# Linear attention with top-1 experts on one core: results of conditional slots moved behind the next branch, three more row buffers, tail weights asked for later

## The chip, the cores and the metric

The kernel runs on one core of a Trainium2 chip. Five engines work side by side, each through its own list of instructions in order: PE (TensorE, the matrix multiplier), ACT (ScalarE), DVE (VectorE), POOL (GpSimd) and SP (SyncE, which here issues the transfers from and to DRAM). An engine that waits for a semaphore holds up everything behind it in its own list. The metric is the device time of one execution in microseconds; the figure of the kernel before is the median of three runs.

## The reference

Attention with positive features is computed for 8 batches, 8 heads and 576 tokens of width 64. Each of the resulting 4608 rows of 512 numbers then goes through one of 8 experts, the one with the largest gate logit.

```python
def phi(x):
    proj = np.einsum('bhsd,df->bhsf', x, w_phi)
    proj = proj - np.max(np.abs(proj), axis=-1, keepdims=True)
    return np.concatenate([np.exp(proj), np.exp(-proj)], axis=-1)
q_p, k_p = (phi(q), phi(k))
kv = np.einsum('bhsf,bhsd->bhfd', k_p, v)
z = np.sum(k_p, axis=2)
num = np.einsum('bhsf,bhfd->bhsd', q_p, kv)
den = np.einsum('bhsf,bhf->bhs', q_p, z)[..., None] + 1e-06
x = num / den                      # 4608 rows of 512
...
logits = x @ w_gate + modality_bias[modality_id]
e_idx = np.argmax(logits, axis=1)
...
for e in range(E):
    mask = e_idx == e
    out[mask] = gate_w[mask, None] * (np.maximum(x[mask] @ w1[e], 0.0) @ w2[e])
```

All is float32. Each expert has weights of 512x1024 and 1024x512, 4 MB together. How many rows an expert gets is known only when the gate has been computed.

## The kernel before, in words

**Attention** runs over 16 quarter groups. Its steps stand in one hand-written list (`ORDER`), under which the lists of SP, PE, ACT and DVE are made. The last step of a block of 128 tokens is `rows()`: DVE multiplies the transposed result by the reciprocal denominators into a buffer `xs` of 128x512 (line 645; `xs_l` is the leftover block of a group), and SP stores it to the DRAM array `x` (line 650). These buffers come from the pool `x1`, which has two of them.

**Routing** counts the rows of each expert and writes lists of (gate weight, row number) to DRAM. The work is cut into *slots* of 256 rows of one expert. Slots 0 to 13 always run. Slots 14 to 20 stand in nested branches `if n > p` (line 1031), where n comes out of the routing; here slots 0 to 17 run. Four small slots are interleaved in slots 6 to 12; the remaining rows of an expert would go into further *small slots*, in branches of their own (`small()`, line 1039 on). With these inputs there is none: the first of their branches jumps over all of them.

**A slot** (`two(p)`) does the following. Weights and tokens are float32, and each is split into a high and a low part, so that a product is made of three matmuls. PE does 96 matmuls of the first layer (line 807), 0.12 us apart, then eight transposes of the next slot's tokens (line 780), then 48 matmuls of the second layer (line 824), 0.23 us apart. Ahead of that:

- SP asks for the weights in four transfers of 1 MB into the buffers `raw` (line 750; two for each layer). A pair is asked for again when its buffers have been split: the second layer's pair of slot p+1 and the first layer's pair of slot p+2 are asked for in slot p. ACT casts the high part (line 770), DVE subtracts the low part (line 772, `l<-raw,h`).
- `mload` lets SP read a slot's list of rows, `me<-lst` (line 724), two slots ahead. `gather` lets POOL fetch these rows, `xg<-x,me` (line 728), once PE has transposed what was in the buffer before.
- At the end, in `second`, DVE scales the two halves of the result by the gate weight into `os` (line 855), and POOL scatters each to the output (`scatter`, line 734).

The weights of small slots go into buffers of their own. `sload(0)` and `sload(1)`, 4 MB each, are asked for just ahead of slot 13. At line 1031 and at line 1039 each engine evaluates the branch by itself, from the counts that it has loaded into its registers. Where a branch is not entered, an engine still performs the semaphore steps that the others rely on.

Of the kernel before, what the change touches and what calls it, by code (L numbers as in the profile page):

```python
# [8 lines left out]
F32 = mybir.dt.float32  # L9
F32R = mybir.dt.float32r  # L10
BF16 = mybir.dt.bfloat16
I32 = mybir.dt.int32
U32 = mybir.dt.uint32
AF = mybir.ActivationFunctionType
ALU = mybir.AluOpType
AX = mybir.AxisListType
PSUM = bass.MemoryType.PSUM
SP, PE, ACT, DVE, POOL = (getattr(mybir.EngineType, e) for e in ("SP", "PE", "Activation", "DVE", "Pool"))

P = 128  # L20
# [5 lines left out]
D, E, F = 512, 8, 1024  # L26
# [6 lines left out]
EARLY, SURE, MOST = 6, 14, 21  # L33
FIX = (1, 3)
FIRST = 6
NME = 8
# [17 lines left out]
class Line:  # L54


    def __init__(self, tc):
        self.tc, self.last, self.free = tc, None, []
# [279 lines left out]
class Attention:  # L338
# [3 lines left out]
    def __init__(self, tc, ci, c, w_phi):  # L342
        self.tc, self.nc = tc, tc.nc
        nc = tc.nc
        self.st, self.rd, self.lg = {}, {}, {}
        self.wp = c.tile([P, P], F32, name="wp")
        for j, e in enumerate((nc.scalar, nc.gpsimd)):
            e.dma_start(self.wp[64 * j:64 * j + 64], w_phi)
        self.c, self.ident = c, ci.tile([P, P], F32, name="ident")
# [291 lines left out]
    def rows(self, T, r0, xp, rd, w, x):  # L641

        nc = self.nc
        xs = w.tile([P, 2, 4, 64], F32, tag="xs", name=f"xs{T}")
        nc.vector.tensor_tensor(xs, xp.rearrange("p (i g d) -> p i g d", i=2, d=64),  # L645
                                rd.rearrange("p g i -> p i g").unsqueeze(3).to_broadcast([P, 2, 4, 64]), ALU.mult)
        xs = xs.rearrange("p i g d -> p (i g d)")
        for j, r in enumerate(r0):
            m = P // len(r0)
            nc.sync.dma_start(x[r:r + m, :], xs[m * j:m * j + m])  # L650
# [39 lines left out]
def run(stages):  # L690
    for _ in stages:
        pass


class Experts:
# [131 lines left out]

    def two(self, p):

        j = p - FIRST  # L830
        for k in range(4):
            if j % 2 == 0 and 0 <= j < 2 * sum(FIX):
                self.fixed(j // 2, k)
            run(self.mm1(k))
            self.wsplit(p, 4 + k)
            next(self.side, None)
            if p < 4:
                next(self.side, None)
        self.wload(p + 1, 1)
        if p + 1 < MOST:  # L840
            self.turn(self.XG)
            run(self.xsplit())
        self.xload(p + 2)
        for t in range(2):
            run(self.second(p, t))
        self.wload(p + 2, 0)

    def second(self, p, t):

        nc, me = self.nc, self.ME[p % NME]  # L850
        pp = self.mm2(p, t)
        yield
        for j in range(2):
            self.wsplit(p + 1, 2 * t + j)
        nc.vector.tensor_scalar(self.OS[t], pp, me[:, t, 0:1].bitcast(F32), None, ALU.mult)  # L855
        self.scatter(me[:, t, 1:2], self.OS[t], D)
        next(self.side, None)
        yield

    def raws(self, s):  # L860

# [138 lines left out]
    def slots(self):  # L1000
        tc, nc = self.tc, self.nc
        why = "the plan makes it within these bounds"
        for p in range(1, SURE):
            j, odd = divmod(p - FIRST + 2, 2)
            if p in range(SURE - 6, SURE - 2):
                for s in range(2):
                    self.smeta(2 * (p - SURE + 6) + s)
            if p == FIRST - 2:
                for i in range(sum(FIX)):
                    self.fmeta(i)  # L1010
            if 0 <= j < sum(FIX):
                self.fload(j, odd)
                if not odd:
                    self.fgather(j)
            if p == SURE - 2:
                self.n, *self.others = (
                    nc.values_load(self.route.n[0:1, i:i + 1], min_val=a, max_val=b, skip_runtime_bounds_check_because=why)
                    for i, a, b in ((0, SURE, MOST), (1, 0, E), (2, 0, E), (3, 0, E)))
            if p == SURE - 1:
                for s in range(2):  # L1020
                    self.sload(s)
                for s in range(3):
                    self.gather(self.rows(s), self.MS[:, 0, s, 1:2])
            self.two(p)
            if 0 <= j < sum(FIX) and odd:
                self.turn(self.HX.unsqueeze(1))
                self.xplain()
            if p == SURE - 1:
                self.turn(self.rows(0).unsqueeze(1))
                self.xplain()  # L1030
        with ExitStack() as st:
            for p in range(SURE, MOST):
                st.enter_context(tc.If(self.n > p))
                self.two(p)

    def small(self):
        tc = self.tc
        more, ones, halves = self.others
        with ExitStack() as st, tc.manual_schedule(engines={SP, PE, ACT, DVE, POOL}):
            for s in range(E):  # L1040
                st.enter_context(tc.If(more > s))
                for t in (3, 4) if s == 0 else (s + 2,) if 3 <= s < E - 2 else ():
                    self.gather(self.rows(t), self.MS[:, 0, t, 1:2])
                if s == 0:
                    with tc.If(more > 3):
                        self.sload(3)
                with tc.If(ones > s) as k:
                    self.one(s)
                with k.Else():
                    with tc.If(halves > s) as k:  # L1050
                        self.part(s, 2)
                    with k.Else():
                        self.part(s, 4)
                if s + 4 < E:
                    with tc.If(more > s + 4):
                        self.sload(s + 4)
# [50 lines left out]
def program(tc, qT, kT, vm, vt, w_phi, w_gate, mod, bias, w1, w2, out):  # L1107
    nc = tc.nc

    def pool(stack, name, side="left", bufs=1, space=bass.MemoryType.SB):  # L1110
        return stack.enter_context(tc.tile_pool(name=name, bufs=bufs, side=side, space=space, reuse_waits="tile"))

    with ExitStack() as ctx:
# [3 lines left out]
        c = pool(ctx, "c")  # L1117
        left, lkv, right, feat, pl, pr, split = (ExitStack() for _ in range(7))
        rw = pool(left, "rw")
        att = Attention(tc, c, pool(left, "ac"), w_phi)  # L1120
# [3 lines left out]
        ex = Experts(tc, att.ident, route, lst, x, w1, w2, out)  # L1124
        ex.ME = [c.tile([P, 2, 2], I32, name=f"me{i}") for i in range(NME)]
        ex.XG = c.tile([P, 2, D], F32, name="xg")
        ex.MS = c.tile([P, 3, E, 2], I32, name="ms")
        ex.MG = c.tile([P, sum(FIX), 2], I32, name="mg")
        ex.IX = [c.tile([P, 1], I32, name=f"ix{i}") for i in range(2)]
        x1 = pool(left, "x1", bufs=2)  # L1130
# [93 lines left out]
        for j, (u, q) in enumerate(order):  # L1224
            k = seen[u, q] = seen.get((u, q), 0) + 1
# [9 lines left out]
        with tc.manual_schedule(engines={SP, PE, ACT, DVE}):  # L1235
# [9 lines left out]
            for j, o in enumerate(order):  # L1245
# [17 lines left out]
                    ex.OS = [b_.tile([P, D], F32, name=f"os{i}") for i in range(2)]  # L1263
                if j == end["lkv"]:
                    lkv.close()
                if o[0] in ("W4", "W5", "W6", "W7") and "h2" not in ex.W:
                    ex.weights(pool(split, "mC", "right"), ("h2", "l2"))
                step(*o)
# [60 lines left out]
```

## Time and profile before

| | us |
|---|---|
| device time, median of 3 runs | 800.19 |
| lowest and highest of these | 799.51, 800.84 |
| the profiled execution | 793.71 |
| its span, first to last instruction | 791.9 |

In the profiled execution PE was busy for 752.0 us, DVE for 552.6, ACT for 449.6 and POOL for 278.9; the mean granted clock of PE was 0.988 of full speed. The kernel read 144.97 MB and wrote 19.55 MB. Attention with the routing fills the first 336 us or so, the slots the rest. The page's times are in microseconds; a row of a timeline has the start, the length, the engine, the line, the operation with output and inputs and, in brackets, how long the engine stood idle before it and what ended that. Rows with SPq, POOLq, DVEq and the like are those of an engine's instruction sequencer: transfers asked for, semaphores and branches. A gap in the sequence of PE's rows costs time only if nothing later would have waited anyway.

### The profile page before, as it was taken

How to read it: one execution, taken by the hardware profiler on the slowest of the kernel's cores; microseconds unless marked ns; L12 is line 12 of the kernel's file. 1: busy time of each engine (PE TensorE's matmuls, PEld its weight loads, DVE VectorE, ACT ScalarE, POOL GpSimd, SP SyncE). 2: the span in 40 equal slices, each digit the busy share in tenths (PEclk: the TensorE clock that was granted, in tenths of full speed). 3: DMA queues.
4: the chain of work that ended last, by engine and by line, in shares of the span. 5: the costliest groups of instructions: out<-in, count | busy, mean ns of one | idle time of the engine just before them, and what ended most of it. 6: DMA issues, size and time to landing. Idle time of an engine off the chain costs nothing. (4 is left out here: it accounts for less than half of the span.)

```text
span 791.9 us, 18459 instructions
## 1 busy us (share of the span) xinstructions
PE 752.0 (95%) x7332; PEld 581.5 (73%) x7332; DVE 552.6 (70%) x815; ACT 449.6 (57%) x675; POOL 278.9 (35%) x163
## 2 busy tenths in 40 slices
PE   6899999989989999979999999999999999989994
PEld 4456555546555555869999987988999889879993
DVE  4889987988788996969765673566546746545752
ACT  3888688767768787535453453445434544435450
POOL 3543434445774784242221231132132321222221
PEclk9999999999999999999999999999999999989997
DMA  8444343336574517669657984867787949956540
GB/s 235 119 119 138 85 138 111 112 101 183 99 133 94 145 28 245 206 198 352 215 199 285 402 314 134 347 217 288 275 304 252 361 164 409 412 183 248 201 174 29
DMA packets 56676, 163.39 MB, mean 206 GB/s; under 512 B 22057, under 2 KB 24173, under 8 KB 43776
## 3 DMA queue, kind: packets, MB, share of 16 engines
q1 hardware_dynamic: 47584, 142.42, 53.7%
q0 software_dynamic: 7792, 18.96, 6.8%
q8 instruction: 62, 1.02, 0.6%
q10 hardware_dynamic: 1200, 0.68, 0.4%
q14 instruction: 38, 0.31, 0.1%
HBM read 144.97 MB, written 19.55 MB: 208 GB/s over the span
## 5 line engine op out<-in xcount | busy, mean ns | idle before, releaser
L770 ACT CAST h<-raw 128x1024 fp32r<-128x1024 f32 x148 | 149.8, 1050 | 107.6 <-PE p L824 56.6
L772 DVE TENSOR_TENSOR l<-raw,h 128x1024 fp32r<-128x1024 f32 x148 | 175.6, 1221 | 47.0 <-ACT h L770 34.4
L502 POOL PARTITION_ALL_REDUCE mq<-d x32 | 129.2, 4040 | 127.5 <-ACT d L476 74.0
L807 PE MATMUL p<-xh,l 128*128 128x256 f32 x576 | 163.9, 285 | 2.8 <-DVE l L772 2.8
L807 PE MATMUL p<-xh,h 128*128 128x256 f32 x576 | 164.7, 287 | 1.1 <-DVE xs L645 1.1
L807 PE MATMUL p<-xl,h 128*128 128x256 f32 x576 | 163.5, 284 | 0.0
L807 PEld LDWEIGHTS p<-xh,l 128*128 128x128 f32 x576 | 110.9, 193 | 5.1 <-DVE l L772 3.0
L807 PEld LDWEIGHTS p<-xh,h 128*128 128x128 f32 x576 | 111.0, 193 | 2.9 <-DVE xs L645 1.3
L728 POOL DMA_INDIRECT xg<-x,me x40 | 55.3, 1383 | 160.7 <-PE pt L780 80.0
L807 PEld LDWEIGHTS p<-xl,h 128*128 128x128 f32 x576 | 111.1, 193 | 0.4
L811 ACT ACTIVATE hh<-p 128x512 fp32r<-128x512 f32 x72 | 42.7, 594 | 112.8 <-PE p L807 112.8
L824 PE MATMUL p<-h,hh 128*128 128x512 f32 x272 | 105.9, 398 | 0.0
L813 DVE SCALAR_TENSOR_TENSOR hl<-p,hh 128x512 fp32r<-128x512 f32 x72 | 49.4, 688 | 80.9 <-ACT hh L811 80.9
L824 PE MATMUL p<-l,hh 128*128 128x512 f32 x272 | 104.3, 392 | 0.0
L824 PE MATMUL p<-h,hl 128*128 128x512 f32 x272 | 104.1, 393 | 0.0
L510 ACT ACTIVATE qp<-d 128x1152 f32<-128x1152 f32 x64 | 71.1, 1161 | 16.8 <-DVE d L505 14.5
L734 POOL DMA_INDIRECT out_dram<-os,me x36 | 39.8, 1106 | 113.7 <-DVE os L855 85.3
L459 ACT ACTIVATE kp<-dk 128x1024 f32<-128x1024 f32 x64 | 64.5, 1063 | 5.2 <-DVE dk L455 5.1
L555 DVE TENSOR_TENSOR kp<-kp 128x1024 f32<-128x1024 f32 x48 | 66.5, 1391 | 0.9 <-PE kvT L522 0.8
L522 PE MATMUL kvT<-kp,va 128*32 128x256 f32 x1024 | 59.2, 380 | 3.9 <-DVE xs L645 1.8
L824 PEld LDWEIGHTS p<-h,hl 128*128 128x128 f32 x272 | 51.5, 189 | 11.0
L824 PEld LDWEIGHTS p<-l,hh 128*128 128x128 f32 x272 | 51.6, 190 | 10.4
(251 smaller groups left out, 1119.8 us busy)
## 6 DMA issues: line engine op xcount, KB each, us to landing
raw<-in_w_dram SPq DMA_DIRECT2D x100, 1024.0 KB
qt<-in_qT_dram SPq DMA_DIRECT2D x30, 288.0 KB
va<-in_vm_dram SPq DMA_DIRECT2D x16, 512.0 KB
x<-xs SPq DMA_DIRECT2D x32, 256.0 KB
kt<-in_kT_dram SPq DMA_DIRECT2D x15, 512.0 KB
kt<-in_kT_dram SPq DMA_DIRECT2D x16, 64.0 KB
vb<-in_vt_dram SPq DMA_DIRECT2D x16, 64.0 KB
x<-xs_l SPq DMA_DIRECT2D x8, 128.0 KB
```

The source lines that it names most:

```text
L459: nc.scalar.activation(kp[:, :, :, s, :].rearrange("p t a f -> p a t f"), dk, AF.Exp, scale=sc)
L502: self.line(nc.gpsimd.partition_all_reduce(mq.rearrange("p a s -> p (a s)"), d.rearrange("p a s -> p (a s)"), P, bass_isa.ReduceOp.absmax))
L510: nc.scalar.activation(q["qp"][:, 2 * pr:2 * pr + 2, i, :], d, AF.Exp, scale=sc)
L522: nc.tensor.matmul(pt[pr][32 * c:32 * c + 32], va[:, pr, t, 32 * c:32 * c + 32], kp[:, pr * 4 + t, c // 2, :, :], start=t == 0, stop=False ...
L555: nc.vector.tensor_tensor(kv4[:, :, t], kv4[:, :, t], kv4[:, :, u], ALU.add)
L728: g = self.nc.gpsimd.indirect_dma_start(xg, None, self.x[:rows, :], IndirectOffsetOnAxis(ix.bitcast(U32), 0), bounds_check=rows - 1, oob_i ...
L770: nc.scalar.copy(h, r)
L772: nc.vector.tensor_tensor(l, r, h, ALU.subtract)
L807: nc.tensor.matmul(pp[:, j], a[:, cc, f], b[:, cc], start=i == 0, stop=i == 11)
L811: nc.scalar.activation(self.HH[:, sl], pp, AF.Relu)
L813: nc.vector.scalar_tensor_tensor(self.HL[:, sl], pp, 0.0, self.HH[:, sl], ALU.max, ALU.subtract)
L824: nc.tensor.matmul(pp, a[:, f, tk], b[:, f], start=i == 0, stop=i == 23)
```

## The change

Three edits, in the words of the code:

1. When the pools that attention's value loads used are closed, a new pool `xo` with three buffers is opened on their place. From then on `rows()` counts its calls, and three calls out of five take a buffer of `xo`, two one of the old pair. What is written and stored is the same.
2. From slot 13 on the last part of a slot, the two `os` rows and their scatters, is no longer written at the end of the slot but in a function `result` that is called at the start of the next slot, behind that slot's branch. The last slot that runs has its results in `small()`, in both ways of its branch: ahead of the small slots if there are some, and in the `Else` if there are none. There the slot's number is not known, so each slot from 13 on copies its list, 128x4 words, to a tile `ml`.
3. `sload(0)` is called after slot 13's `two`, `sload(1)` inside the branch for small slots, if there are more than one of them.

```diff
@@ rows
+        if self.out:
+            self.turns += 1
+            if self.turns % 5 > 1:
+                w = self.out[0]
         xs = w.tile([P, 2, 4, 64], F32, tag="xs", name=f"xs{T}")
...
@@ two
+        if p >= SURE - 1:
+            for t in range(2) if p >= SURE else ():
+                self.result(self.ME[(p - 1) % NME], t)
+            self.nc.vector.tensor_copy(self.ML, self.ME[p % NME])
...
@@ second
-        nc.vector.tensor_scalar(self.OS[t], pp, me[:, t, 0:1].bitcast(F32), None, ALU.mult)
+        if p < SURE - 1:
+            self.result(me, t)
+        next(self.side, None)
+        yield
+
+    def result(self, me, t):
+        self.nc.vector.tensor_scalar(self.OS[t], self.P2[t], me[:, t, 0:1].bitcast(F32), None, ALU.mult)
         self.scatter(me[:, t, 1:2], self.OS[t], D)
-        next(self.side, None)
-        yield
...
@@ slots
             if p == SURE - 1:
-                for s in range(2):
-                    self.sload(s)
                 for s in range(3):
                     self.gather(self.rows(s), self.MS[:, 0, s, 1:2])
             self.two(p)
...
             if p == SURE - 1:
                 self.turn(self.rows(0).unsqueeze(1))
                 self.xplain()
+                self.sload(0)
...
@@ small
+        with self.tc.manual_schedule(engines={SP, PE, ACT, DVE, POOL}):
+            with self.tc.If(self.others[0] > 0) as k:
+                for t in range(2):
+                    self.result(self.ML, t)
+                self.lists()
+            with k.Else():
+                for t in range(2):
+                    self.result(self.ML, t)
+
+    def lists(self):
         tc = self.tc
         more, ones, halves = self.others
-        with ExitStack() as st, tc.manual_schedule(engines={SP, PE, ACT, DVE, POOL}):
+        with ExitStack() as st:
             for s in range(E):
-                st.enter_context(tc.If(more > s))
+                if s:
+                    st.enter_context(tc.If(more > s))
...
-                    with tc.If(more > 3):
-                        self.sload(3)
+                    for t in (1, 3):
+                        with tc.If(more > t):
+                            self.sload(t)
...
@@ program
                 if j == end["lkv"]:
                     lkv.close()
+                    att.out.append(pool(left, "xo", bufs=3))
```

How the lists of the engines change is shown at three places. The first is DVE's list around the end of slot 0 (`os` of slot 0; `raw_0` and `raw_2` are weights of slot 1; `ns4l`, `al`, `cetl` belong to the routing). Before:

```order
L855 TENSOR_SCALAR os_3927<-pt_3869,me_73 128x512
L219 TENSOR_TENSOR ns4l<-ns4l,fi4l 128x8
L219 TENSOR_TENSOR al<-tri,ns4l 128x8x8
L645 TENSOR_TENSOR xs_0_4337<-xp_0_4254,rd_4_4071 128x512
L241 TENSOR_REDUCE cetl<-al 128x8
L645 TENSOR_TENSOR xs_l<-xl_4262,rd_8_4076 128x512
L772 TENSOR_TENSOR l_3862<-raw_0_123,h_3861 128x1024 x2
```

After:

```order
L869 TENSOR_SCALAR os_3928<-pt_3870,me_73 128x512
L649 TENSOR_TENSOR xs_0_4341<-xp_0_4258,rd_4_4075 128x512
L649 TENSOR_TENSOR xs_l<-xl_4266,rd_8_4080 128x512
L776 TENSOR_TENSOR l_3863<-raw_0_124,h_3862 128x1024 x2
L219 TENSOR_TENSOR ns4l<-ns4l,fi4l 128x8
L219 TENSOR_TENSOR al<-tri,ns4l 128x8x8
L776 TENSOR_TENSOR l_4058<-raw_2_3967,h_4057 128x1024 x2
```

The two `xs` rows moved up behind `os`, and the weight splits up behind them; the routing rows now stand later.

The second is SP's list in slot 13; the transfers of weights come in pairs, and one row of each pair stands here. `raw_0_123` and `raw_2_3963` (after: `raw_0_124` and `raw_2_3967`) are the weights of the slots, the `raw` with a last number from 4391 to 4402 those of small slots, `me_80` is the list of slot 15. Before (slot 15's first pair follows):

```order
L750 DMA raw_0_123<-in_w_dram 128x2048
...
L750 DMA raw_0_4391<-in_w_dram 128x2048
...
L750 DMA raw_2_4393<-in_w_dram 128x2048
...
L750 DMA raw_0_4395<-in_w_dram 128x2048
...
L750 DMA raw_2_4397<-in_w_dram 128x2048
...
L750 DMA raw_2_3963<-in_w_dram 128x2048
...
L724 DMA me_80<-lst 128x2x2
```

After:

```order
L754 DMA raw_0_124<-in_w_dram 128x2048
...
L754 DMA raw_2_3967<-in_w_dram 128x2048
...
L728 DMA me_80<-lst 128x2x2
...
L754 DMA raw_0_124<-in_w_dram 128x2048
...
L754 DMA raw_0_4396<-in_w_dram 128x2048
...
L754 DMA raw_2_4398<-in_w_dram 128x2048
```

The list and slot 15's first pair now come ahead of the small slots' weights, of which two pairs are left.

The third is the border of slots 13 and 14 on DVE (`me_78` is the list of slot 13, line 1031 and 1042 the branch of slot 14). Before:

```order
L855 TENSOR_SCALAR os_3926<-p_4411,me_78 128x512
L855 TENSOR_SCALAR os_3927<-p_4412,me_78 128x512
L1031 COMPARE_AND_BRANCH
L772 TENSOR_TENSOR l_4054<-raw_2_3963,h_4053 128x1024 x2
L772 TENSOR_TENSOR l_4054<-raw_3_3964,h_4053 128x1024 x2
```

After:

```order
L1042 COMPARE_AND_BRANCH
L869 TENSOR_SCALAR os_3927<-p_4416,me_78 128x512
L869 TENSOR_SCALAR os_3928<-p_4417,me_78 128x512
L837 COPY ml<-me_79 128x4
L776 TENSOR_TENSOR l_4058<-raw_2_3967,h_4057 128x1024 x2
L776 TENSOR_TENSOR l_4058<-raw_3_3968,h_4057 128x1024 x2
```

The two results of slot 13 moved behind the branch, and the copy of slot 14's list was added. On POOL the same was done with the scatters; at the end of POOL's list, where the branches of slots 14 to 20 close, the last of them and what follows was, before:

```order
L1031 COMPARE_AND_BRANCH
L757 COMPARE_AND_BRANCH
L757 UNCONDITIONAL_BRANCH x2
L734 DMA out_dram<-os_3926,me_77 4608x512
L734 DMA out_dram<-os_3927,me_77 4608x512
L1031 UNCONDITIONAL_BRANCH
```

and is after, with the flags and the branch of the small slots ahead of the scatters:

```order
L1042 ISA
L1042 UNCONDITIONAL_BRANCH
L1029 TENSOR_LOAD nslots x3
L1049 COMPARE_AND_BRANCH
L738 DMA out_dram<-os_3927,ml 4608x512
L738 DMA out_dram<-os_3928,ml 4608x512
```

The scatters that stood ahead of the closing branches stand behind them.

## Rows read from the trace of the kernel before

**Rows 1.** The page, part 1: busy us (share of the span) xinstructions.

```profile
PE 752.0 (95%) x7332; PEld 581.5 (73%) x7332; DVE 552.6 (70%) x815; ACT 449.6 (57%) x675; POOL 278.9 (35%) x163
```

**Rows 2.** Slots 1, 2, 13, 14: length, busy, PEclk, DMA share, GB/s.

```profile
347.60:377.10 29.50, 25.57 (x156) 23.23 (x155) 26.45 (x85) 11.35 (x14) 6.63 (x7) 0.94 0.76 268
377.10:400.40 23.30, 23.30 (x153) 21.33 (x152) 18.52 (x34) 11.36 (x14) 5.59 (x4) 1.00 0.67 232
656.40:679.66 23.26, 23.26 (x154) 21.30 (x154) 11.73 (x15) 8.04 (x11) 2.11 (x3) 1.00 1.01 417
679.66:710.02 30.36, 26.34 (x155) 23.57 (x154) 14.44 (x16) 14.94 (x19) 6.75 (x6) 0.89 0.75 287
```

**Rows 3.** DVE timeline, slot 1: start, us, operation [idle before <-releaser].

```profile
342.36 0.75 DVE L855 TENSOR_SCALAR os<-pt,me 128x512 f32<-128x512 f32 x1 [0.26 <-PE pt L824]
...
349.18 0.69 DVE L645 TENSOR_TENSOR xs<-xp,rd 128x512 f32<-128x512 f32 x1 [5.81 <-DMA x<-xs]
...
351.46 0.69 DVE L645 TENSOR_TENSOR xs_l<-xl,rd 128x512 f32<-128x512 f32 x1 [1.47 <-DMA x<-xs]
352.07 2.35 DVE L772 TENSOR_TENSOR l<-raw,h 128x1024 fp32r<-128x1024 f32 x2
```

**Rows 4.** Timeline of PE in slot 1.

```profile
349.93 0.39 PE L807 MATMUL p<-xh,h 128*128 128x256 f32 x1 [1.12 <-DVE xs L645]
...
353.34 0.58 PE L807 MATMUL p<-xh,l 128*128 128x256 f32 x1 [2.80 <-DVE l L772]
```

**Rows 5.** Timeline of SP's DMA issues, 318 to 360 us.

```profile
326.33 6.14 SPq L650 DMA_DIRECT2D x<-xs  x3
...
337.16 13.06 SPq L650 DMA_DIRECT2D x<-xs  x3
```

**Rows 6.** Timeline of SP's DMA issues, 640 to 700 us.

```profile
646.70 15.78 SPq L750 DMA_DIRECT2D raw<-in_w_dram  x12
665.53 0.38 SPq L724 DMA_DIRECT2D me<-lst  x1
670.07 18.77 SPq L750 DMA_DIRECT2D raw<-in_w_dram  x4
```

**Rows 7.** Timeline of POOL, slot 14.

```profile
686.34 1.82 POOL L728 DMA_INDIRECT xg<-x,me  x1 [4.45 <-PE p L807]
```

**Rows 8.** Timeline of PE, slot 14.

```profile
693.88 0.30 PE L780 MATMUL pt<-ident,xg 128*128 128x128 f32 x1 [2.47 <-DMA xg<-x,me]
695.74 1.76 PE L780 MATMUL pt<-ident,xg 128*128 128x128 f32 x7 [1.55 <-DMA xg<-x,me]
```

**Rows 9.** Timeline of DVE, last 20 us.

```profile
773.44 1.28 DVE L790 TENSOR_TENSOR xl<-pt,xh 128x512 fp32r<-128x512 f32 x2
779.26 0.75 DVE L855 TENSOR_SCALAR os<-p,me 128x512 f32<-128x512 f32 x1 [4.54 <-PE p L824]
780.17 0.75 DVE L855 TENSOR_SCALAR os<-p,me 128x512 f32<-128x512 f32 x1 [0.16 <-PE p L824]
```

**Rows 10.** Timeline of POOL, last 32 us.

```profile
771.88 1.93 POOL L728 DMA_INDIRECT xg<-x,me  x1 [0.31 <-issue]
...
781.61 0.99 POOL L734 DMA_INDIRECT out_dram<-os,me  x1 [0.30 <-issue]
```

**Rows 11.** Line 1031: count, ns min/median/max, first and last start.

```profile
L1031 DVEq COMPARE_BRANCH  x6: 43/45/63, 679.5 to 781.1; - x6
...
L1031 POOLq EVENT_SEMAPHORE  x4: 17/43/3859, 781.1 to 785.2; - x4
...
L1031 POOLq INC_SWDGE_SEM  x1: 492/492/492, 785.3 to 785.3; - x1
```

**Rows 12.** Line 1039, the branch around the small slots.

```profile
L1039 DVEq COMPARE_BRANCH  x1: 56/56/56, 782.7 to 782.7; - x1
...
L1039 DVEq EVENT_SEMAPHORE  x1: 21/21/21, 786.0 to 786.0; - x1
```

**Rows 13.** Line 1325, the end of the program.

```profile
L1325 SPq EVENT_SEMAPHORE  x14: 17/28/28, 789.7 to 791.8; - x14
```

More of the change, by code (lines that the diff above doesn't have):

```diff
@@ L344, in __init__ @@
         nc = tc.nc
-        self.st, self.rd, self.lg = {}, {}, {}
+        self.st, self.rd, self.lg, self.out, self.turns = {}, {}, {}, [], 0
         self.wp = c.tile([P, P], F32, name="wp")
@@ L854, in second @@
             self.wsplit(p + 1, 2 * t + j)
-        nc.vector.tensor_scalar(self.OS[t], pp, me[:, t, 0:1].bitcast(F32), None, ALU.mult)
-        self.scatter(me[:, t, 1:2], self.OS[t], D)
+        if p < SURE - 1:
+            self.result(me, t)
         next(self.side, None)
         yield
+    def result(self, me, t):
+        self.nc.vector.tensor_scalar(self.OS[t], self.P2[t], me[:, t, 0:1].bitcast(F32), None, ALU.mult)
+        self.scatter(me[:, t, 1:2], self.OS[t], D)
     def raws(self, s):
@@ L1127, in program @@
         ex.MS = c.tile([P, 3, E, 2], I32, name="ms")
+        ex.ML = c.tile([P, 2, 2], I32, name="ml")
         ex.MG = c.tile([P, sum(FIX), 2], I32, name="mg")
```

## The prediction

> **What bounds the kernel now.** I read the busy table first: TensorE (PE) works in 95% of the span [rows 1], so only the places where PE is not fed can give anything back. The stage table by slot shows them: slot 2 and slot 13 take 23.30 and 23.26 us with PE busy all the time, while slot 1 takes 29.50 us with 25.57 busy and slot 14 takes 30.36 with 26.34 busy, both at a lower granted clock (0.94, 0.89) [rows 2]. A third place is the end: the last result leaves VectorE (DVE) at about 780.9, and the span runs to 791.9 [rows 9]. Everything else between 336 and 780 us is a row of 23.3 us slots that touch each other. The change edits the three places, so I price each by itself.
>
> **Slot 1: three more buffers.** The timeline of DVE has two idle stretches there: 5.81 us before the row `xs` at 349.18 and 1.47 us before `xs_l` at 351.46, both put down to the DMA `x<-xs` [rows 3]. DVE wants to write a buffer that an earlier store has not yet left. The store rows of SyncE (SP) show why: three stores start at 337.16 and are spread over 13.06 us [rows 5]. Behind the two `xs` rows in DVE's order stand two weight splits `l<-raw,h` (352.07, 2.35 us) [rows 3], and PE waits for these: 1.12 us at 349.93 for `xs` and 2.80 us at 353.34 for `l`, where the matmul takes 0.58 us [rows 4]; the whole slot has 0.94 of the clock [rows 2]. In the changed order `xs_0` and `xs_l` stand right behind `os`, then the splits, and the small routing rows come later. Without the wait DVE needs 342.36+0.75 for `os`, 0.69+0.69 for the two `xs`, 2.35 for the splits: done at 346.8, ahead of 347.60, where slot 1's first matmul ran. The gain is slot 1 against slot 2: 29.50-23.30 = 6.2 us [rows 2]. Slot 1 holds three matmul records more than slot 2 (transposes, some 0.3 us), which stay: **5.9 us**. The lower bound is the two idle stretches alone, 1.12+2.80 = 3.9 [rows 4], the upper 6.2. The buffers that the last two `xs` now take were last stored from in the group that starts at 326.33 [rows 5]. As I read the rotation of two buffers, the wait that ended at 349.18 was for a store of the group from 337.16, so that store took at most 12 us; 326.33+12 = 338.3, before 343. What is late next in slot 1? The casts and gathers have no idle row of PE in this stretch but the two named. The cover of the moved routing rows is DVE's own slack: in slot 2 it is busy 18.52 of 23.30 us [rows 2].
>
> **Slot 14: 8 MB asked for later.** PE stands 2.47 us and 1.55 us for the token gathers `xg<-x,me` of slot 15 (693.88, 695.74) [rows 8], then starts on the lower clock: the stretch has 0.89, slot 13 had 1.00 [rows 2]. The gather itself begins only at 686.34 [rows 7], since its list of tokens `me<-lst` is asked for by SP at 665.53, behind one run of twelve 1 MB weight loads that began at 646.70 [rows 6]. Slot 13, in which they land, moves 417 GB/s with the DMA engines busy in all of it [rows 2]; 12 MB at that rate is 30 us. Eight of the twelve are for small slots, of which none runs here (between the last scatter and the end there is no work of one). After the change the order of SP is: four loads for slot 14, the list, two loads for slot 15, then four tail loads; the other four stand in a branch that is not taken. The list may still be asked for at about 665, when the buffers of its forerunners come free, but it is behind 4 MB in place of 12: 8 MB or 20 us at 417 GB/s sooner. A list that lands near 670 in place of 686 lets the gather land near 678 (it took 693.88-686.34 = 7.5 us), and PE wants its data at 691. The wait of 4 us and the slow start go: 30.36-23.30 = 7.06, **7.0 us**. Lower bound: the idle alone, 2.47+1.55 = 4.0. Of the moved part, the four remaining loads (4 MB, 10 us at 417 GB/s) now stand between slot 15's first and second pair of weights. The first pair is released from about 670 (SP's four loads from 670.07 [rows 6]), so 8 MB take 20 us and end near 690; the second pair is first needed in slot 15's expansion, 703 at the new pace, and the next list has until about 714. I cost the move at nothing because these 13 us cover it; without that cover PE would wait for it microsecond by microsecond.
>
> **The conditional slots: results behind the branch.** Removed: nothing. Added: one DVE copy of 128x4 words in each of five executed slots. No row shows it; it lies between nothing and the 0.75 us of the 128x512 `os` [rows 3], much nearer to nothing, and even 0.75 is hidden, since DVE is busy 14.44 of 30.36 us in slot 14 [rows 2]: 0 on PE's path. Moved: two `os` rows and two scatters per slot go past each engine's branch. The accumulators that they read are written again only in the next slot's second half, 11 us later, so a delay there is hidden. On POOL the gather of the slot after next no longer stands behind scatters of the same slot but behind those of the slot before: nothing is later. On SP nothing moves.
> What counts is the end. Before, POOL issues the last scatter at 781.61 (0.99 us) [rows 10]. Behind it one of its semaphore rows takes 3.86 us from 781.1, as I read it the wait for the data to land (785.0), and one step of 0.49 us follows [rows 11]; then come the exit branch, three flags and a second branch. SP's closing rows begin only at 789.7 and end at 791.8 [rows 13]. So from landing (about 785.0) to the closing there are 4.7 us of branches, and these now run before the results, while PE still does slot 17's second half. For POOL the work ahead of the branches is a gather issued at 771.88 at the latest; allow it the 3.4 us that the scatter took from issue to landing, then 4.7 us of branches: 780.0 [rows 10], just when the first `os` is ready. For DVE: its last work before the results ends at 773.44+1.28 = 774.72 [rows 9], and the way from the exit branch (781.1 [rows 11]) to the end of the second jump (786.0 [rows 12]) took 4.9 us: 779.6, against a result at 779.26 [rows 9], 0.3 us late. The second scatter may have one semaphore step of 0.45 to 0.5 us ahead of it. The landing is then 785.0 to 785.8, plus the closing 2.2 us (789.7 to 791.9): 787.2 to 788.0. I take 787.5: **4.4 us**. Upper bound 5.4 (no delay, and part of the closing overlapped), lower 1.0 (below).
> A taken branch can be long here: DVE's second one took 782.7 to 786.0, 3.3 us [rows 12], while the exit branch on DVE showed 0.06 us at most [rows 11]. The Trainium skill, "Runtime: NRT & Kernel Launch", section "Instruction fetch mechanics", says that a taken branch whose target lies outside the loaded window must fetch its page first. By that rule both taken branches could stall on DVE; the trace shows it for one of the two. What it would make of the end is rival B.
>
> **The sum.** 5.9+7.0+4.4 = 17.3 us. The profiled execution took 793.71 us with a span of 791.9; it would have 774.6 of span and 776.4 in all. The median of the runs is 800.19, 6.5 us above the profiled one; none of the three places is known to differ between them, so the same 17.3 come off it: 782.9 us.
>
> **Rivals.** A: slot 14's wait is only shifted. The 4 MB now come ahead of the second pair of weights and the list for slot 16; if PE then waits there as it does now (4 us and a slow start, 7.0), the sum is 10.3 and the time 789.9; a half of it gives 786.4. For: the DMA engines were already full at 417 GB/s [rows 2]. Against: 13 us of cover.
> B: the end gives little. If DVE fetches for both taken branches, 3.3 us more, the results start at 783 in place of 779.6, and 4.4 falls to 1.0: 786.3 us. For: the 3.3 us row. Against: the exit branch's short row.
> C: the change does not do what it says: with five turns the old pair still serves two of them, and if those two meet the same store, slot 1 keeps its 5.9: 788.8. Against: the store is ten microseconds older [rows 5].
> D, slower than before: the 8 MB in front of slot 15's second pair of weights starve it. Place: PE in slot 15 waiting for `l`. It costs nothing while 8 MB (8.4 million bytes) pass in 33 us (670 to 703), which is 254 GB/s. To eat all 17.3 us it must take over 50 us, under 167 GB/s. At 150 GB/s, for example, they take 56 us and PE waits 23: 805.9. For: slot 2 moved 232 GB/s [rows 2]. Against: its DMA engines were busy 0.67 of the time, so that was what was asked for; the stretch with queued loads had 417.
>
> **How the numbers follow.** The forecast has 0.62; its own range is 780.0 to 785.5. A 0.11, B 0.12, C 0.06, D 0.05, and 0.04 for gains that are lost in small new waits until nothing remains. Low end: all upper bounds, 6.2+7.1+5.4 = 18.7, and 1.5 us for the runs' own spread: 780. High end: one of A, B, C in full, up to 790. What lies above 790 (two rivals at once, D, none) and below 780 is under 2 in 10. About 0.2%, 1.6 us, is what a measurement of this kernel can tell from no change. All cases but the last two are faster by more: faster 0.91, same 0.04, slower 0.05.
>
> **What would show it.** Slot 1 and slot 14 at 23.3 to 23.6 us in the stage table, without idle rows before `xs` and `xg`; about 4 MB less read; the list of slot 15 asked for 2 us behind slot 14's second pair; `os` of slot 17 within 0.5 us of PE's last matmuls; 7 us from the last `os` to the end of the span in place of 11. I am wrong in the step of slot 14 if PE waits for `raw` or `xg` in slots 15 or 16, in the step of the end if DVE's or POOL's jump ends after PE, and in the step of slot 1 if DVE still waits for `x<-xs`.

## The result, and the profile after

| | before | after |
|---|---|---|
| median of 4 runs each, us | 800.52 (799.51 to 801.43) | 789.22 (789.03 to 790.12) |
| span of the profiled execution, us | 791.9 | 788.3 |
| HBM read, MB | 144.97 | 140.77 |

The ratio is 0.9861, with a 95% interval of 0.9844 to 0.9879: 11.3 us faster. The forecast was 17.3 us (782.9 us, range 780 to 790). So the direction and the range held, and a third of the gain is missing. Medians here and below hold every execution, ratios leave out two that lie far from all others (1073.96 us in e3, 2499.61 us of the kernel before). The spans differ by only 3.6 us, although the profile shows all three places mended. The stage table of the changed kernel, cut at the same four slots as [rows 2] (columns: length, then busy time of PE, PEld, DVE, ACT and POOL, granted clock, DMA share, GB/s):

```profile
358.28:383.07 24.79, 23.91 (x157) 21.75 (x155) 22.67 (x76) 13.37 (x17) 6.61 (x7) 1.00 1.02 309
383.07:406.02 22.95, 22.95 (x150) 21.04 (x149) 18.93 (x38) 11.36 (x14) 5.69 (x4) 1.00 0.71 241
663.29:686.96 23.67, 23.67 (x158) 21.70 (x156) 12.16 (x16) 8.19 (x11) 5.07 (x5) 1.00 0.71 255
686.96:710.35 23.39, 23.39 (x156) 21.48 (x154) 14.34 (x17) 14.63 (x19) 4.02 (x4) 1.00 0.95 368
```

Slot 1 went from 29.50 to 24.79 us and slot 14 from 30.36 to 23.39, both now at full clock. DVE's timeline at the end of slot 0 shows how: the rows that answer to [rows 3] follow each other without a wait, in the order that was read from the list.

```profile
353.04 0.75 DVE L869 TENSOR_SCALAR os<-pt,me 128x512 f32<-128x512 f32 x1 [0.24 <-PE pt L828]
353.71 0.68 DVE L649 TENSOR_TENSOR xs<-xp,rd 128x512 f32<-128x512 f32 x1
354.31 0.68 DVE L649 TENSOR_TENSOR xs_l<-xl,rd 128x512 f32<-128x512 f32 x1
354.90 2.35 DVE L776 TENSOR_TENSOR l<-raw,h 128x1024 fp32r<-128x1024 f32 x2
```

One gap is left in slot 1, which stood in no row before. PE's timeline:

```profile
360.37 0.33 PE L784 MATMUL pt<-ident,xg 128*128 128x128 f32 x1 [0.88 <-DMA xg<-x,me]
```

SP's transfers and POOL's first gather around slot 14, which answer to [rows 6, 7]: four weight loads, then the list, and only then the tail loads, in one run of eight with the slots' own. The gather is at 676.00, 11 us ahead of slot 14.

```profile
654.00 12.38 SPq L754 DMA_DIRECT2D raw<-in_w_dram  x4
667.28 0.16 SPq L728 DMA_DIRECT2D me<-lst  x1
677.39 16.34 SPq L754 DMA_DIRECT2D raw<-in_w_dram  x8
```

```profile
676.00 1.04 POOL L732 DMA_INDIRECT xg<-x,me  x1 [9.11 <-PE pt L784]
```

The end, as in [rows 9 to 13]. PE's last matmul, DVE's last rows, POOL's last scatter, and by source line (count, ns min/median/max, first and last start) the branches and the closing:

```profile
780.06 0.39 PE L828 MATMUL p<-h,hl 128*128 128x512 f32 x1
```

```profile
773.76 1.28 DVE L794 TENSOR_TENSOR xl<-pt,xh 128x512 fp32r<-128x512 f32 x2
780.85 1.41 DVE L869 TENSOR_SCALAR os<-p,ml 128x512 f32<-128x512 f32 x2 [5.81 <-PEq L1042]
```

```profile
783.20 0.99 POOL L738 DMA_INDIRECT out_dram<-os,ml  x1 [0.31 <-DMA xg<-x,me]
```

```profile
L1042 PEldq EVENT_SEMAPHORE  x1: 51/51/51, 780.7 to 780.7; - x1
...
L1049 DVEq COMPARE_BRANCH  x1: 56/56/56, 776.9 to 776.9; - x1
L1049 POOLq COMPARE_BRANCH  x1: 45/45/45, 778.2 to 778.2; - x1
...
L1350 SPq EVENT_SEMAPHORE  x14: 17/28/3454, 783.2 to 788.2; - x14
```

DVE's and POOL's branches of the small slots (776.9, 778.2) now lie ahead of the results, and from the last `os` (ends at 782.26) to the end of the span there are 6.0 us where there were 11.0. What took the gain back lies where the change touches nothing. Slot 0's second layer starts at 336.59 us in the trace of before and at 347.28 in this one:

```profile
336.59 0.50 PE L824 MATMUL pt<-h,hh 128*128 128x512 f32 x1 [0.27 <-DVE xl L790]
```

```profile
347.28 0.49 PE L828 MATMUL pt<-h,hh 128*128 128x512 f32 x1 [0.27 <-issue]
```

By the first two rows of the table below, the three places gave 4.7+7.0+3.9 = 15.6 us. The 10.7 us of attention took most of that, and slots 8 and 10 another 1.3: cut in the same way, they are 29.20 and 28.33 us long here and 28.09 each before.

### The profile page after: what moved, and what is told of

It reads as the page before. It is cut to its first block, busy times and chain, and to the rows that moved or that the text cites. A ratio compares the mean times of both kernels' runs of the same rounds, so it can differ in the third digit from the quotient of the medians.

```text
span 788.3 us, 18445 instructions
## 1 busy us (share of the span) xinstructions
PE 755.1 (96%) x7332; PEld 581.6 (74%) x7332; DVE 552.9 (70%) x820; ACT 449.0 (57%) x675; POOL 279.5 (35%) x163
## 3 DMA queue, kind: packets, MB, share of 16 engines
HBM read 140.77 MB, written 19.55 MB: 203 GB/s over the span
## 5 line engine op out<-in xcount | busy, mean ns | idle before, releaser
L828 PEld LDWEIGHTS p<-l,hh 128*128 128x128 f32 x272 | 51.1, 188 | 10.3
```

The source lines that it names most:

```text
L828: nc.tensor.matmul(pp, a[:, f, tk], b[:, f], start=i == 0, stop=i == 23)
```

## The experiments

The runs of three later sessions stand beside runs of the kernel before of the same session: medians of 792.65, 793.88 and 792.56 us there, against 800.52 at first. This table is worked out from PE's timeline in each trace: where slot 0's second layer starts; slots 1 and 14, from the end of the last second-layer matmul of the slot before to that of its own (by this cut slot 14 of before is 30.72 us); and the end, which is counted to the end of the span from 0.23 us (the spacing of these matmuls) behind the start of PE's last one.

| trace | slot 0 | slot 1 | slot 14 | end | span |
|---|---|---|---|---|---|
| before, on record | 336.59 | 29.51 | 30.72 | 11.93 | 791.9 |
| after, on record | 347.28 | 24.79 | 23.75 | 8.01 | 788.3 |
| e1, before again | 340.18 | 29.17 | 26.03 | 11.94 | 790.5 |
| e2, rows only | 338.69 | 23.70 | 27.71 | 12.07 | 785.3 |
| e3, weights only | 337.71 | 29.37 | 23.75 | 12.09 | 786.1 |
| e4, results only | 337.89 | 29.63 | 28.50 | 7.22 | 786.4 |
| e5, after again | 337.91 | 23.69 | 23.75 | 7.52 | 776.0 |
| e6, before filled | 337.57 | 30.39 | 29.91 | 11.75 | 792.8 |
| e7, after filled | 337.06 | 23.70 | 23.75 | 7.54 | 775.2 |
| e8, list early | 339.48 | 30.23 | 23.76 | 12.25 | 788.9 |
| e9, after, third time | 339.54 | 23.69 | 23.74 | 7.50 | 777.6 |
| e10, store late | 345.95 | 23.69 | 23.74 | 7.78 | 784.3 |
| e11, rows early | 338.32 | 23.69 | 23.74 | 7.71 | 776.6 |

**The kernel before, a second trace.** Nothing is edited.

> The kernel before, unchanged, for a second trace. In the trace on record PE stands 3.28 us at 166.9 and runs on at the full granted clock; the changed kernel stands as long at the same place and runs on at 0.5 to 0.67, and reaches slot 0 about 10.7 us later. Theory 'clock': that is chance of an execution, and a usual execution of the kernel before also drops its clock there; then this trace shows a granted clock under 0.8 in 168 to 176 us, slot 0 starts 4 to 11 us later than 336.6, and the span is near 798 to 800. Rival 'change': the kernel before keeps its clock always and the change makes attention slower; then this trace has 1.00 there, the second layer of slot 0 starts at 336.6 and the span is near 792.

Measured: 792.35 us, span 790.5. Slot 0 starts 3.6 us later than in the trace on record, just short of the 4 to 11 that were expected, and the granted clock of the stretch from 160 to 180 us is 0.83, not 1.00 (0.62 from 168 to 176). The stage tables of that stretch, first of before on record, then of this trace:

```profile
160.00:180.00 20.00, 16.72 (x243) 9.59 (x244) 17.24 (x28) 13.77 (x22) 9.57 (x4) 1.00 0.42 113
```

```profile
160.00:180.00 20.00, 16.73 (x203) 9.42 (x205) 15.06 (x24) 12.57 (x19) 9.82 (x4) 0.83 0.32 86
```

PE was busy as long, but did 203 matmuls in place of 243: 1.00 is the full 2.4 GHz, and a mean of 0.83 says that part of the stretch ran at the lower level of 1.2. PE had stood as long just before in both traces, here on record and then again:

```profile
170.22 0.63 PE L656 MATMUL rp<-ident,dn 128*128 128x128 f32 x4 [3.28 <-DVE dn L602]
```

```profile
170.46 1.08 PE L656 MATMUL rp<-ident,dn 128*128 128x128 f32 x4 [3.27 <-DVE dn L602]
```

So the kernel before, too, can lose its clock there. The expected span (798 to 800) was missed: slot 14 takes only 26.03 us here, 4.7 less than on record. Its wait is no constant.

**Each part by itself.** First the three buffers alone.

```diff
...
+        if self.out:
+            self.turns += 1
+            if self.turns % 5 > 1:
+                w = self.out[0]
         xs = w.tile([P, 2, 4, 64], F32, tag="xs", name=f"xs{T}")
...
                     lkv.close()
+                    att.out.append(pool(left, "xo", bufs=3))
```

> Only the three more buffers. Theory 'local': slots 1 and 2 together get shorter by 4.8 us (52.5 to 47.7 as in the changed kernel), slot 14 stays at 30.4, the end at 11.9 us after PE's last matmul; 795.5 us, ratio 0.994. Rival 'shared': the new pool is what slows attention (other addresses, other order), then the gain of 4.8 is given back ahead of slot 0 and the ratio is 0.998 to 1.002.

Measured: 788.06 us against 792.65, ratio 0.9928 (0.9896 to 0.9960). Its stage rows for slots 1 and 14:

```profile
349.73:373.43 23.70, 23.70 (x157) 21.75 (x156) 23.00 (x77) 11.46 (x14) 6.26 (x7) 1.00 1.02 329
675.58:703.29 27.71, 25.75 (x158) 23.17 (x157) 14.60 (x17) 14.82 (x19) 6.00 (x6) 0.94 0.81 318
```

PE is busy in all of slot 1, which is 5.8 us shorter than in the trace of before on record. Slot 0 starts at 338.69, between the two traces of the kernel before, which is no sign that the new buffers slow attention. Then the tail weights alone:

> Only the tail weights asked for later. Theory 'local': slot 14 goes from 30.4 to 23.4 us, slot 1 and the end stay; 793.5 us, ratio 0.991. Rival 'shared': the wait moves to slot 15 or 16 or to the end, at most half of 7 us stays; 796.5 or more.

```diff
             if p == SURE - 1:
-                for s in range(2):
-                    self.sload(s)
...
                 self.xplain()
+                self.sload(0)
...
-                    with tc.If(more > 3):
-                        self.sload(3)
+                    for t in (1, 3):
+                        with tc.If(more > t):
+                            self.sload(t)
```

Measured: 791.05 us, ratio 0.9983 (0.9956 to 1.0010). Slot 14 is at 23.75 us in the trace, as the theory says:

```profile
680.32:704.07 23.75, 23.75 (x158) 21.83 (x156) 14.45 (x17) 14.65 (x19) 4.08 (x4) 1.00 0.94 370
```

The median gained 1.6 us, though, and not 7: by the interval it is 3.5 at most. The trace is of the shortest of the ten executions (787.98 us), so it does not show where the longer ones lost time. And the results alone, with both `sload` calls where they were:

```diff
...
+        if p >= SURE - 1:
+            for t in range(2) if p >= SURE else ():
+                self.result(self.ME[(p - 1) % NME], t)
+            self.nc.vector.tensor_copy(self.ML, self.ME[p % NME])
...
-        nc.vector.tensor_scalar(self.OS[t], pp, me[:, t, 0:1].bitcast(F32), None, ALU.mult)
-        self.scatter(me[:, t, 1:2], self.OS[t], D)
+        if p < SURE - 1:
+            self.result(me, t)
...
+            with self.tc.If(self.others[0] > 0) as k:
+                for t in range(2):
+                    self.result(self.ML, t)
+                self.lists()
+            with k.Else():
+                for t in range(2):
+                    self.result(self.ML, t)
```

> Only the results behind the next branch. Theory 'local': from PE's last matmul to the end of the span 8.0 us in place of 11.9, nothing else moves; 796.5 us, ratio 0.995. Rival 'shared': the new tile moves the addresses of what is allocated behind it, and with that attention gets some 4 us slower; then 800 us, ratio 1.000.

Measured: 788.18 us, ratio 0.9939 (0.9899 to 0.9978). The end is 7.22 us, 4.7 shorter, and DVE's results come in one row right behind PE's exit step, as in the changed kernel:

```profile
779.52 1.41 DVE L865 TENSOR_SCALAR os<-p,ml 128x512 f32<-128x512 f32 x2 [5.60 <-PEq L1039]
```

In the traces, each edit mends its own place and no other. In medians the three parts sum to 4.6+1.6+4.5 = 10.7 us, less than the whole kernel gains below; with intervals of 2 to 3 us on each part, whether the rest is more than scatter stays open.

**The changed kernel, a second and a third trace.**

> The changed kernel, unchanged, on the chip of these runs. In its trace on record slot 0 starts 10.7 us later than in that of before: PE's clock fell at 170 us (0.83 in 160 to 180, as in the second trace of the kernel before, 3.6 us), and a second stretch follows at 237 to 242 where DVE stood 2.26 us before an xs row (0.94 in 220 to 250). Theory 'clock and chance': the second stretch is chance too; here slot 0 starts between 336.6 and 341, the slots and the end stay as in the trace on record (slot 1 at 24 to 25 us, slot 14 at 23.8, 8.0 us of end), the span is 777 to 782, the median 780 to 784 and the ratio 0.985. Rival 'change': the changed kernel always meets the second stretch; slot 0 starts at 345 or later again, the span is near 788 and the ratio 0.99 or more.

> The changed kernel, unchanged, for a third trace and beside the next two. Theory 'chance': attention and the routing cost what they cost in the second trace, the second layer of slot 0 starts at 337 to 341, 777 to 782 us, ratio 0.98. Rival 'change': the late start of the first trace (347.3) comes back, 789 us.

Measured: 777.73 us, ratio 0.9795 (0.9759 to 0.9831), and 779.22 us, ratio 0.9825 (0.9798 to 0.9851). That is 16.2 and 13.3 us off the runs of before beside them; the first of the two is faster than was expected (780 to 784). Slot 0 starts at 337.91 and 339.54, and slot 1 takes 23.69 us, without the gap for `xg`. The late start of the first trace is no property of the changed kernel. The stage rows of the second trace of after, with PE fully busy through all of slots 1 and 14:

```profile
348.93:372.62 23.69, 23.69 (x157) 21.73 (x155) 21.80 (x75) 11.36 (x14) 5.82 (x7) 1.00 1.00 321
674.79:698.54 23.75, 23.75 (x158) 21.83 (x156) 14.54 (x18) 14.62 (x19) 4.05 (x4) 1.00 0.93 366
```

**The stand at 167 us filled.** The edit, in `xr`, the same for both kernels:

```diff
+        for t in range(26 if b == 3 else 0):
+            nc.tensor.transpose(rp[:, 0], self.ident, self.ident)
         for t in range(4):
             nc.tensor.transpose(rp[:, t], self.dn[:, self.tile(b, t)], self.ident)
```

> The kernel before with 26 more transposes of the identity on PE at 167 us, where it stands 3.28 us; they take about 3.0 us of that and their output is overwritten. Theory 'clock': the clock stays at 1.00 in 160 to 180, slot 0 starts at 336 to 337 as in the trace of before, 1 to 4 us earlier than in the other traces, and the times lie closer together; ratio 0.996 to 0.998. Rival: the late start has another cause (transfers, POOL), the clock of that stretch only follows; then slot 0 starts at 338 to 341 as without the transposes, ratio 1.000.

> The changed kernel with the same 26 transposes. Theory 'clock and chance': slot 0 at 336 to 337, span 776 to 778, 778 to 780 us, 1 to 4 us ahead of the changed kernel of this call. Rival 'change': the second stretch at 237 us stays, slot 0 at 343 or later, and at most 3.6 us are won against the changed kernel.

Measured: 793.34 us against 793.88, ratio 0.9994 (0.9963 to 1.0024), and 778.42 us, ratio 0.9805 (0.9769 to 0.9841), where the unfilled changed kernel had 777.73. The clock is 1.00 from 160 to 180 us in both traces, and nothing is won in the medians; the interval of the kernel before still allows some 3 us. The start of slot 0 (337.57, 337.06) is within 0.6 us of where my theory had it, but other traces reach 337.7 with a clock of 0.91. Behind the mended stretch the next wait is longer: DVE's `xs` row in the trace of the filled kernel before

```profile
228.39 0.69 DVE L645 TENSOR_TENSOR xs<-xp,rd 128x512 f32<-128x512 f32 x1 [2.81 <-DMA x<-xs]
```

waits 2.81 us for a store, where it was 2.05 in e1. As I read it, part of what the clock costs at 170 us is hidden behind a store that is awaited at 228 anyway. The theory that the clock there explains the 6 us of missing gain falls.

**The list of slot 15, early.** In the kernel before, one transfer is moved and the eight tail loads stay.

```diff
-        if p >= EARLY:
+        if p >= EARLY and p != SURE + 1:
             self.mload(p)
...
+                self.mload(SURE + 1)
                 for s in range(2):
                     self.sload(s)
```

> The kernel before with one transfer moved: the list of slot 15 (2 KB) is asked for ahead of the eight tail loads, which stay where they are. Theory 'list': slot 14 waited for the list behind 12 MB, not for the weights; slot 14 takes 23.3 to 23.8 us as with the tail loads moved, and 2 to 7 us are won (ratio 0.992 to 0.998). Rival 'weights': the 12 MB themselves hold slot 14 up; then PE waits for the weight splits in slot 14 instead and it keeps 26 us or more.

Measured: 790.09 us, ratio 0.9949 (0.9914 to 0.9983). SP's rows, then POOL's:

```profile
653.54 0.38 SPq L724 DMA_DIRECT2D me<-lst  x1
654.44 40.33 SPq L750 DMA_DIRECT2D raw<-in_w_dram  x14
```

```profile
672.35 1.04 POOL L728 DMA_INDIRECT xg<-x,me  x1 [9.11 <-PE pt L780]
```

With all the tail loads still in the way, slot 14 takes 23.76 us. So PE waited for 2 KB behind 12 MB, not for the weights. In the second trace of the kernel before, the gather's row names the list itself, which SP had asked for at 669.20:

```profile
687.95 1.04 POOL L728 DMA_INDIRECT xg<-x,me  x1 [2.78 <-DMA me<-lst]
```

**A store made late.** The changed kernel with two extra reads ahead of one store:

```diff
         xs = xs.rearrange("p i g d -> p (i g d)")
+        if T == "4_0":
+            for j in range(2):
+                nc.sync.dma_start(self.slow[0][j], self.slow[1][0:2 * P, :].rearrange("(p h) c -> p h c", h=2)[:, j])
```

(`slow` is the pair of slot 0's raw buffers and the weights `w1`.)

> The changed kernel with two extra reads of 1 MB each asked for by SP just ahead of one store of a row buffer at about 226 us (into buffers that are loaded again later; nothing is computed from them). They delay that store by some 5 us. Theory 'store': the row two turns on (at 232 us in the second trace of the changed kernel, 237 in the first) waits on DVE for the store, PE runs dry behind it and its clock falls near 240, as in the first trace: slot 0 starts 5 to 9 us later than without, 783 to 787 us, the slots and the end unchanged. Rival 'slack': DVE and PE have other work there; slot 0 starts at most 2 us later, 778 to 780 us.

Measured: 785.79 us, ratio 0.9905 (0.9869 to 0.9941), 6.6 us over the unedited kernel of the same session. DVE's row and PE's behind it:

```profile
240.12 0.69 DVE L649 TENSOR_TENSOR xs<-xp,rd 128x512 f32<-128x512 f32 x1 [6.59 <-DMA x<-xs]
```

```profile
240.86 1.72 PE L578 MATMUL pn<-qp,kv 128*32 128x448 f32 x8 [3.67 <-DVE xs L649]
```

And the stage rows of 220 to 250 us, of this kernel, of the first trace of after and of its second:

```profile
220.00:250.00 30.00, 22.52 (x270) 13.93 (x270) 18.36 (x21) 15.77 (x28) 16.38 (x12) 0.89 0.79 170
```

```profile
220.00:250.00 30.00, 25.09 (x303) 14.88 (x296) 20.47 (x25) 17.27 (x33) 19.40 (x12) 0.94 0.54 108
```

```profile
220.00:250.00 30.00, 26.39 (x370) 15.53 (x370) 23.44 (x27) 20.14 (x32) 21.18 (x13) 1.00 0.77 118
```

A late store in this stretch costs what the theory said: DVE's `xs` row is late, PE stands behind it, the clock falls (0.70 from 240 to 250), and slot 0 starts at 345.95 (347.28 in the first trace), with the slots and the end unchanged. In the first trace that row is at

```profile
237.24 0.69 DVE L649 TENSOR_TENSOR xs<-xp,rd 128x512 f32<-128x512 f32 x1 [2.26 <-issue]
```

with its releaser not recorded, at the same place in DVE's list. But no row of PE there names it. PE's own rows stretch from just ahead of it on, at gaps for which the profile shows no wait, where the third trace (e9) has one `pk` row without a gap. First the rows of the first trace, then that of e9:

```profile
236.85 0.50 PE L449 MATMUL pk<-wp,kt 64*128 64x128 f32 x4 [0.25 <-issue]
238.31 0.27 PE L449 MATMUL pk<-wp,kt 64*128 64x128 f32 x1 [0.96 <-issue]
239.03 0.37 PE L469 MATMUL pe<-wp,kt 64*128 64x128 f32 x1 [0.33 <-issue]
```

```profile
234.47 1.06 PE L449 MATMUL pk<-wp,kt 64*128 64x128 f32 x16
```

Nor does the delay come at one place. Against e9, which has the same clock of 0.83 at 160 to 180 us, DVE in e10 is 6.5 us late from the `xs` row on. In the first trace it is 1.4 us late at 219, 3.7 at the `xs` row, 5.7 at 245, 6.2 at 255 and 7.8 at 286. So it is shown what a late store can cost here. That a store came late in the first session is not shown, and no row ties PE's gaps to one; what made attention slow there stays open.

**One more row buffer from the start.** In the changed kernel, a pool `xe` of one buffer lies in the space of `lkv`, and `rows()` rotates over it and the old pair until the three new buffers come.

```diff
+        self.turns += 1
+        if len(self.out) > 1:
             if self.turns % 5 > 1:
-                w = self.out[0]
+                w = self.out[1]
+        elif self.turns % 3 == 2:
+            w = self.out[0]
...
         odd_k = pool(lkv, "oddk")
+        att.out.append(pool(lkv, "xe"))
```

> The changed kernel with one more row buffer from the start of attention on (in the space that is freed when the three new ones come). DVE's waits for a store at 228 us (1.4 to 2.8 us in the traces) go. Theory 'store': PE's gaps at 226 to 230 us (1.83 and 1.07 to 1.47) get shorter, slot 0 starts 1 to 3 us earlier than in the changed kernel; ratio 0.976 to 0.979 against 0.98. Rival: another wait ends last there (PE waits for the ACT and DVE steps between), slot 0 starts where it did; ratio 0.98.

Measured: 777.32 us, ratio 0.9805 (0.9777 to 0.9832), 1.9 us under the changed kernel of the same session (six runs each: 776.84 to 779.15 and 778.64 to 779.42). DVE's wait at 228 is gone, the two rows touch:

```profile
228.41 1.28 DVE L651 TENSOR_TENSOR xs<-xp,rd 128x512 f32<-128x512 f32 x2
```

Slot 0 starts 1.2 us earlier than in e9. PE's gap of 1.8 us (ahead of 228.64 in e9, of 229.23 here) stays, since it is for the `xs` row itself. This is the fastest version by median in its session, by less than its interval against before can tell.

## Why the prediction was right, and where it was off

**Slot 1: right.** 5.9 forecast; 29.51 to 23.69 or 23.70 us is 5.8 in all six later traces with the buffers. Six traces without them have 29.17 to 30.39 us, 29.7 on the mean, which makes 6.0. Rival C did not come. In the first trace 4.7, since PE met one more wait (0.88 us for `xg`), which the step on what is late next had denied. It came in that trace alone. One reading was short: the stores from 326.33 on are spread over 6.14 us [rows 5], so by the step's own 12 us the last of them could land at 344.5, behind the 343 that it had to beat; DVE's rows show no wait for it.

**Slot 14: right mechanism, one execution's size.** The forecast was 7.0 of [rows 2], and against that trace 30.72 to 23.75 is exactly that. But in five traces with the old order of transfers and the list in its place the slot took 30.72, 26.03, 27.71, 28.50 and 29.91 us, 28.6 on the mean. On the mean the gain is 4.8. The recorded execution was the worst of the five; a wait of PE for a transfer behind 12 MB was read as a constant. The runs are lower still: with the place mended alone, the medians gained 1.6 us (e3, at most 3.5) and 3.8 us (e8). Why e3 gained less than 4.8 stays open. That the move costs nothing was right: slots 15 and 16 of e5 take 23.3 us each, rivals A and D did not come.

**The end: right, by another wait.** 4.4 forecast; 11.93 to 8.01 in the first trace (3.9), to 7.50 and 7.52 in the next ones (4.4). The step had DVE's second jump end at 779.6, some 0.3 us late. In the trace it ended at 779.8, and the rows `os` stood until PE's own exit step of the branch at 780.7 (`PEq L1042` in DVE's row). So both results start only when PE has left the branch, and the results and the scatters follow some 1.0 to 1.3 us later behind PE's last matmul than before (scatter: 783.20-780.06 against 781.61-779.74). PE's last matmul before is

```profile
779.74 0.39 PE L824 MATMUL p<-h,hl 128*128 128x512 f32 x1
```

What made up for it is the closing: in e5, 4.7 us from the start of the last scatter to the end of the span at 776.0, where before it was 10.3.

```profile
771.29 0.99 POOL L738 DMA_INDIRECT out_dram<-os,ml  x1 [0.30 <-DMA xg<-x,me]
```

Rival B did not come: of DVE's two branches, the exit takes 0.06 us at most and only the second is followed by a long jump, 2.9 us (776.9 to 779.8) where it was 3.3 before. The Trainium skill states in "Runtime: NRT & Kernel Launch", section "Instruction fetch mechanics", that a taken branch whose target lies outside the loaded window waits until the target's page is fetched. The trace agrees at the second branch and shows no such wait at the exit; no run here shows whether a fetch is what takes the time.

**The sum: the step that failed is the one that carried it over to the median.** It said that none of the three places was known to differ between the profiled execution of 793.71 us and runs of 800. The difference was real, 6.5 us, and it was put aside. For the profiled execution the same sum gave 776.4 us, and the second trace of the changed kernel is of an execution of 777.88, with 1.3 of the 1.5 us in slot 0's start. Slot 14, whose wait was the longest of five traces in the profiled execution, can hardly be what made the other runs longer, so they most likely lost time elsewhere. The first trace of after shows one such place: attention, 10.7 us against the trace of before. Read from DVE's rows that both have, the changed kernel is 2.7 us later at 183, 3.9 at 219, 8.6 at 245 and 10.7 from 286 us on. Against usual traces of the same kernel (337.9, 339.5) it is 7.7 to 9.4 us. In the first session both kernels were slower than in the later three, before by 6.6 to 8.0 us and after by 10.0 to 11.5, and the gain came out as 11.3. Where attention ran as usual, the gain was 16.2 and 13.3 us; the places sum to 6.0+4.8+4.5 = 15.3 with each at the mean of its traces. That the longer runs of the kernel before lost their time at the same place in attention is argued only: there is no trace of one. The record says this much: of the other 53 runs of the kernel before in the later sessions, 789.8 to 800.7 us long, the seven over 797 us have a mean granted clock of 0.981 to 0.985, the nine under 791 us one of 0.987 to 0.991. So the longer runs spent more time at the lower clock, which would fit attention and slot 14 alike.

That the range held the first result, 789.22, is luck: its upper end was there for rivals A to C, none of which came.

## What to carry to other kernels

A wait for a transfer that stands behind many megabytes should be read from several executions before it is priced: here 2.3 to 7.0 us for the same lines. If the profiled execution is faster than the runs by more than their spread, the difference lies somewhere, and a sum worked out from that execution may not carry over to the runs. A small transfer that an engine needs soon (here a list of 2 KB) is worth asking for ahead of bulk loads in the same queue, and work at a branch's exit is best done while another engine still computes: here that took 3.9 to 4.7 us off the end.

## What the runs showed of the hardware

- The same stand of PE, 3.27 to 3.29 us ahead of 170, had three outcomes. The granted clock of 160 to 180 us was 1.00 in two of the eleven unfilled traces (before on record, e5), 0.91 in four (e2, e3, e4, e10) and 0.83 in five (after on record, e1, e8, e9, e11). Between e5 and e9, the same kernel at 1.00 and 0.83, slot 0 starts 1.6 us apart.
- A delay of one 256 KB store by two reads of 1 MB made DVE stand 6.59 us and the run 6.6 us longer: slot 0 started 6.4 us later than in e9, so at this place, with two buffers, hardly anything hid the late store.
- The results that are computed behind the exit of the branch waited for PE's exit step (780.7, then `os` at 780.85 us; in e4 too DVE's row names it), although the last matmul's row had ended at 780.45.
- A list of 2 KB asked for at 669.20 us behind twelve loads of 1 MB kept its gather waiting until 687.95 (e1). Where it was asked for at 653.54, ahead of the tail loads, the gather started at 672.35 and its row names PE (e8).
